# Order of the first loads in a fused attention and gated-unit kernel: tile 1 alone, the value weights in one piece, tiles 2 and 3 together

## The chip, the cores and the metric

The kernel runs on one core of one Trainium2 chip. The metric is the device time of one execution in microseconds (us). A core has TensorE (PE: matmuls; PEld is its weight load), VectorE (DVE), ScalarE (ACT), GpSimd (POOL) and SyncE (SP), which here does nothing but issue transfers (DMA). The engines run their own instruction lists in order and meet at semaphores.

## The reference

One block over 2048 tokens of 512 features, all in bfloat16:

```python
xn = (x - mean(x)) / sqrt(var(x) + 1e-5)                 # per token
q, k, v = split(xn @ wqkv)                               # 32 heads of 16
pq, pk = q @ w_phi, k @ w_phi                            # per head
phi_q = concat(softmax(pq), softmax(-pq))                # phi_k alike from pk
o = (phi_q @ (phi_k.T @ v)) / (phi_q . sum(phi_k) + 1e-6)
out = x + o @ wo + ((xn @ w_gate) * (xn @ w_up)) @ w_down    # 1792 inner features
```

What bears on the change is the beginning: tokens are centred, transposed, and multiplied by the value columns of `wqkv` (columns 1024 to 1535), by `w_gate` and by `w_up`.

## The kernel before, in words

The tokens are 16 tiles of 128 (`NT`), the gated unit works on 4 groups of 4 tiles, with 14 inner tiles each (`units`, line 737). All data lie in one SBUF tensor named `arena`, all matmul results in one PSUM tensor named `ps`, so most rows of the profile have the same names; shapes and times tell them apart.

**The planner.** The program is not written in the order in which it runs. Helpers (`act_op`, `dve`, `pool`, `mms`, `sc.dma`, lines 157 to 307) record steps with an estimated cost, the ranges that they read and write, and a priority. `_order` (line 819) then plays the steps through: on each engine the step that can start first goes first, and steps marked urgent may pass others. The order of each engine's instructions is fixed there, before the kernel runs; semaphore waits are put in by `_emit_all`. For a transfer, the argument `at` (line 157) is the due time in nanoseconds at which the planner takes its data to be there; it is an assumption, and nothing waits for it on the chip. SP issues its transfers in the order that comes out, which for the first loads is the order of the code.

**The first loads** (lines 366 to 380): tile 0 (128 KB), tiles 1 and 2 (256 KB), rows 0 to 255 of the value weights (256 KB), tile 3 (128 KB), rows 256 to 511 of the value weights (256 KB), four of the fourteen columns tiles of gate and up weights (512 KB each), the small head weights, tiles 4 to 7 (512 KB), the key weights by a transposing DMA, five more column tiles of gate and up weights. Ahead of these, ScalarE issues three tiny transfers (`peek`, line 353) that read a few elements of three weight tensors; their data are used nowhere.

**The four start tiles** (`RAW = 4`). The loop at line 757 records for each of tiles 0 to 3:

- `emit_centred` (line 433): the sum of the token's features, and then `512 * x - sum` as centred tokens, without the division by the standard deviation. For tiles 0, 1 and 3 the sum is a VectorE instruction over the two halves of a row (line 443); for the tile in `ACT_MEAN` (tile 2) it is a ScalarE copy with an accumulator (line 437). The subtraction (line 449) is VectorE's: two instructions of 256 columns for tiles 0 and 1, one of 512 for the others.
- `emit_T` (line 494): four TensorE transposes (matmuls against an identity, 128 columns each) in two pairs, each pair copied from PSUM to SBUF by a ScalarE instruction (line 499).
- `emit_moments` and `emit_root` (lines 429 and 455): variance by VectorE (`bn_stats`, `bn_aggr`), and one over the standard deviation by GpSimd. It is applied later, as the scale of ScalarE's copies (`scale_of`).
- `k_pe` (line 574): four value matmuls of 512 columns, one for each quarter of the features. Quarters 0 and 1 read the first half of the value weights, quarters 2 and 3 the second.

While the first tokens are on their way TensorE runs 28 matmuls on constants (line 384), and four more behind tile 0's transposes (line 764).

**Behind the start.** `glu` (line 607) records four gate matmuls and four up matmuls for each of its units; they take tokens of a whole group, so the first of them needs all four start tiles and the gate weights. Then come the key weights' product with the head weights (`wprime(1)`), the key features, the sums over tokens (`emit_kv`), the query side and the output (`final`).

Of the kernel before, what the change touches and what calls it, by code (L numbers as in the profile page):

```python
# [12 lines left out]
PE, ACT, DVE, POOL, SP = "PE", "ACT", "DVE", "POOL", "SP"  # L13
# [168 lines left out]
def bass_parallel_sum__linear_kernel_hedgehog__glu_gated_bilinear__prompt_kernel(  # L182
    nc: bass.Bass,
    A_x: bass.AP,
    A_wqkv: bass.AP,
    A_w_phi: bass.AP,
    A_wo: bass.AP,
    B_x: bass.AP,
    B_w_gate: bass.AP,
    B_w_up: bass.AP,  # L190
    B_w_down: bass.AP,
    out: bass.AP,
):
    with ExitStack() as es:
        _build(nc, es, A_x, A_wqkv, A_w_phi, A_wo, B_w_gate, B_w_up, B_w_down, out)


def _build(nc, es, A_x, A_wqkv, A_w_phi, A_wo, B_w_gate, B_w_up, B_w_down, out):
# [60 lines left out]
    def sbv(name, lo, n):  # L259
        off = layout[name] + lo  # L260
        return arena[:, off:off + n]

    def sbf(name, lo_f32, n_f32):
        off = layout[name]
        return arena[:, off:off + 2 * (lo_f32 + n_f32)].bitcast(F32)[:, lo_f32:lo_f32 + n_f32]
# [21 lines left out]
    def dve(fn, reads, writes, n, rate=1.0, fixed=65.0, prio=None):  # L287
        return sc.step(DVE, fn, reads=reads, writes=writes, cost=fixed + rate * n / 0.96, lat=150.0, prio=prio)
# [31 lines left out]
    def x_tile(t):  # L320
        return sbv("x", t * 512, 512)
# [7 lines left out]
    wv_v = sbv("wv", 0, NQ * 512).rearrange("p (q j) -> p q j", q=NQ)  # L329
# [7 lines left out]
    def load_x(on, t0, n, at):  # L337
        return sc.dma(on, sbv("x", t0 * 512, n * 512).rearrange("p (t d) -> p t d", t=n),
                      x_flat[t0 * 128:(t0 + n) * 128, :].rearrange("(t p) d -> p t d", p=128), at=at)

    def load_w(on, dst, src, at, issue=500.0):
        return sc.dma(on, dst, src, at=at, issue=issue)
# [5 lines left out]
    def load_gu(on, f0, n, at, up=None):  # L348
        return [load_w(on, v[:, :, f0 * 128:(f0 + n) * 128],
                       src[:, f0 * 128:(f0 + n) * 128].rearrange("(q p) f -> p q f", p=128), to)  # L350
                for v, src, to in ((wg_v, B_w_gate, at), (wu_v, B_w_up, up or at))]
# [12 lines left out]
    st = peek(2, every_8th(B_w_up, 0))  # L364

    load_x(SP, 0, 1, 2950.0)
    def load_v(h, at):
        return load_w(SP, wv_v[:, 2 * h:2 * h + 2, :],
                      A_wqkv[h * 256:(h + 1) * 256, 1024:1536].rearrange("(q p) j -> p q j", p=128), at)

    load_x(SP, 1, 2, 3850.0)
    load_v(0, 5050.0)
    load_x(SP, 3, 1, 6100.0)
    load_v(1, 7000.0)
    load_gu(SP, 0, 4, 8300.0, 10600.0)
    sc.dma(SP, wphi_v, bass.AP(tensor=A_w_phi.tensor, offset=A_w_phi.offset, ap=[[16, 128], [2048, NQ], [1, 16]]),
           at=10700.0)
    load_x(SP, 4, 4, 12100.0)
# [45 lines left out]

    RAW = 4

    ACT_MEAN = (2,)

    def emit_moments(t):
        dve(lambda e: e.bn_stats(stats_v[:, t, 0:6], x_tile(t)), [x_tile(t)], [stats_v[:, t, 0:6]], 512)  # L430
# [2 lines left out]
    def emit_centred(t):  # L433

        total = lnt_v[:, 1, 8 + t:9 + t]
        if t in ACT_MEAN:
            sc.step(ACT, lambda e: e.activation(out=xn_tile(t), in_=x_tile(t), func=ACTF.Copy, accum_out=total),
                    reads=[x_tile(t)], writes=[xn_tile(t), total], cost=700.0, lat=180.0)
            again = [xn_tile(t)]
        else:  # L440
            pairs = sbf("tree", (t % 2) * 256, 256)
            lo, hi = x_tile(t)[:, 0:256], x_tile(t)[:, 256:512]
            dve(lambda e: e.scalar_tensor_tensor(out=pairs, in0=lo, scalar=1.0, in1=hi, op0=ALU.mult, op1=ALU.add,  # L443
                                                 accum_out=total), [x_tile(t)], [pairs, total], 256, fixed=150.0)
            again = [pairs]
        n = 256 if t in (0, 1) else 512
        for c in range(0, 512, n):
            o, i = xn_tile(t)[:, c:c + n], x_tile(t)[:, c:c + n]
            dve(lambda e, o=o, i=i: e.tensor_scalar(out=o, in0=i, scalar1=float(D), scalar2=total, op0=ALU.mult,
                                                    op1=ALU.subtract), again + [i, total], [o], n, rate=0.5)  # L450
# [32 lines left out]
    def xn_tile(t):  # L483
        return sbv("xn", (t % 4) * 512, 512)
# [272 lines left out]
    for t in range(RAW):  # L757
        first = len(sc.steps)
        emit_centred(t)
        emit_T(t)  # L760
        for st in sc.steps[first:]:
            st.urgent = True
        if t == 0:
            mms([(bank(3, 0, 128), one, one, True, True)] * 4, cold=True).deps.append(sc.by_eng[PE][-2])
        emit_moments(t)
        emit_root(t)
        k_pe(t)
# [189 lines left out]
```

## Time and profile before

| | |
|---|---|
| runs shown | 219.54, 219.38, 219.1 us; median 219.38 |
| profiled execution | 219.1 us, its span 217.9 us |
| busy share of the span | TensorE 98%, VectorE 86%, ScalarE 59%, GpSimd 5% |
| read from HBM, written | 8.67 MB, 2.10 MB |
| granted TensorE clock | 1.00 |

Times in the profile count from the span's start. A row of the timeline has the start, the duration, the engine, the line, the operation, what it writes and reads, the shapes and how many instructions are merged; in brackets stands how long the engine was idle before it, and what ended the wait. A transfer's time is told from its issue to its landing, the moment at which all its data are there. TensorE's matmuls overlap: one of 512 columns is shown with 0.38 us, and the next one starts 0.216 us after it.

### The profile page before, as it was taken

The page shows a single profiled execution, that of the slowest core. Times are in us where ns is not written, and L with a number is a line of the kernel's source. Part 1 is how long each engine was busy: PE and PEld are TensorE (multiplying, and loading weights), DVE is VectorE, ACT ScalarE, POOL GpSimd, SP SyncE. Part 2 cuts the span into 40 slices and gives each one's busy share as a digit, 9 for nine tenths or more (in the row PEclk, how much of TensorE's full clock was granted, in tenths as well). Part 3 has the DMA queues.
Part 4 walks back from the last instruction along what each step waited for, and adds up shares of the span by engine and source line. Part 5 has one row for each costly group of instructions (what it writes and reads, how often), then busy time and mean ns, then how long its engine had stood idle before and what let it go on. Part 6 is the DMA issues. An engine that isn't in the chain of part 4 may idle for free.

```text
span 217.9 us, 3623 instructions
## 1 busy us (share of the span) xinstructions
PE 213.2 (98%) x1291; PEld 104.4 (48%) x1314; DVE 187.1 (86%) x556; ACT 128.7 (59%) x223; POOL 10.8 (5%) x29
## 2 busy tenths in 40 slices
PE   7999999999999999999999999999999999999996
PEld 6444444444444554444446444444445444454544
DVE  3785999999999549999998799999999999995512
ACT  4668966548553399999884899795254531110000
POOL 2432000110000300000000000000000000000000
PEclk9999999999999999999999999999999999999999
DMA  5994690025900224000000005542681746447321
GB/s 167 321 280 106 164 317 5 0 48 130 350 5 2 47 52 96 0 0 3 0 2 3 2 0 96 76 93 51 122 138 34 167 99 145 97 98 148 90 56 48
DMA packets 47698, 19.92 MB, mean 91 GB/s; under 512 B 37696, under 2 KB 47680, under 8 KB 47680
## 3 DMA queue, kind: packets, MB, share of 16 engines
q1 hardware_dynamic: 47440, 19.69, 37.8%
q8 instruction: 10, 0.16, 0.3%
q14 instruction: 8, 0.07, 0.1%
q10 hardware_dynamic: 240, 0.00, 0.1%
HBM read 8.67 MB, written 2.10 MB: 49 GB/s over the span
## 4 chain that ended last, share of the span: by engine, by line
PE 95%; DMA 2%; SPq 1%; issue 1%; DVE 0%
PE ps L298 95%; DMA arena<-in_A_wqkv_dram 2%; SPq L165 1%; DVE arena L732 0%
## 5 line engine op out<-in xcount | busy, mean ns | idle before, releaser
L298 PE MATMUL ps<-arena 128*128 128x512 bf16 (+5 forms) x1259 | 209.8, 327 | 2.0 <-issue 0.3
L298 PEld LDWEIGHTS ps<-arena 128*128 128x128 bf16 (+1 forms) x1282 | 101.2, 98 | 110.7 <-ACT arena L278 1.6
L278 ACT ACTIVATE arena<-ps 128x512 bf16<-128x512 f32 (+2 forms) x168 | 86.9, 632 | 38.2 <-PE ps L298 26.4
L278 ACT ACTIVATE arena<-arena 128x1024 bf16<-128x1024 bf16 (+1 forms) x40 | 39.6, 1005 | 21.0 <-DVE arena L550 20.8
L564 DVE TENSOR_TENSOR arena<-arena 128x64 f32<-128x64 f32 (+3 forms) x128 | 49.8, 401 | 0.3 <-ACT arena L278 0.2
L544 DVE TENSOR_TENSOR arena<-arena 128x64 bf16<-128x64 bf16 (+3 forms) x128 | 32.0, 276 | 3.8 <-ACT arena L278 3.4
L550 DVE TENSOR_TENSOR arena<-arena 128x1024 bf16<-128x1024 bf16 x32 | 21.7, 680 | 0.1
L625 DVE TENSOR_TENSOR arena<-ps,arena 128x512 bf16<-128x512 f32 x28 | 19.0, 680 | 0.8 <-PE ps L298 0.8
L732 DVE TENSOR_TENSOR arena<-ps,arena 128x512 bf16<-128x512 f32 (+2 forms) x13 | 8.4, 645 | 9.3 <-PE ps L298 9.0
L622 DVE TENSOR_TENSOR arena<-arena 128x512 bf16<-128x512 bf16 x28 | 11.7, 417 | 4.1 <-ACT arena L278 3.9
L596 DVE TENSOR_TENSOR arena<-arena 128x1024 bf16<-128x1024 bf16 x16 | 11.0, 685 | 0.1
L472 DVE BATCH_NORM_STATS2 arena<-arena 128x6 f32<-128x512 bf16 x12 | 8.1, 686 | 1.6 <-DMA arena<-in_A_x_dram 1.6
L278 ACT ACTIVATE arena<-ps,arena 128x512 bf16<-128x512 f32 x12 | 8.0, 682 | 2.1 <-POOL arena L459 1.0
L593 DVE RECIPROCAL arena<-arena 128x64 bf16<-128x64 f32 x16 | 8.8, 549 | 0.0
L694 DVE RECIPROCAL arena<-ps 128x32 f32<-128x32 f32 x16 | 5.6, 348 | 3.3 <-PE ps L298 3.3
L702 DVE TENSOR_TENSOR arena<-ps,arena 128x512 bf16<-128x512 f32 x12 | 8.2, 685 | 0.1
L681 DVE TENSOR_TENSOR arena<-arena 128x512 bf16<-128x512 bf16 x16 | 6.7, 419 | 0.0
L678 DVE RECIPROCAL arena<-arena 128x32 f32<-128x32 f32 x16 | 5.6, 349 | 0.0
L503 DVE TENSOR_SCALAR arena<-arena 128x512 bf16<-128x512 bf16 x12 | 4.2, 408 | 0.9 <-POOL arena L480 0.8
L298 PE MATMUL ps<-const-bfloat16-1.0 128*128 128x128 bf16 x32 | 3.5, 298 | 0.8 <-PEq L942 0.8
L478 POOL TENSOR_SCALAR arena<-arena 128x4 f32<-128x4 f32 x3 | 1.6, 518 | 54.6 <-DVE arena L474 54.6
L443 DVE SCALAR_TENSOR_TENSOR arena<-arena 128x256 f32<-128x256 bf16 x3 | 1.3, 425 | 3.4 <-DMA arena<-in_A_x_dram 3.2
(33 smaller groups left out, 36.0 us busy)
## 6 DMA issues: line engine op xcount, KB each, us to landing
out_dram<-arena SPq DMA_DIRECT2D x15, 128.0 KB, 2.0
arena<-in_B_w_down_dram SPq DMA_DIRECT2D x1, 1792.0 KB, 7.5
arena<-in_B_w_gate_dram SPq DMA_DIRECT2D x2, 640.0 KB, 6.0
arena<-in_B_w_up_dram SPq DMA_DIRECT2D x2, 640.0 KB, 7.9
arena<-in_A_x_dram SPq DMA_DIRECT2D x1, 1024.0 KB, 6.3
arena<-arena SPq DMA_TRANSPOSE x44, 2.6
arena<-in_A_wqkv_dram SPq DMA_DIRECT2D x2, 256.0 KB, 3.8
arena<-in_B_w_gate_dram SPq DMA_DIRECT2D x1, 512.0 KB, 5.3
```

The costliest lines, as they stand in the source:

```text
L278: return e.activation(out=out_ap, in_=in_ap, func=func, scale=scale, **kw)
L298: ins = e.matmul(o, lhsT=l, rhs=r, start=a, stop=z)
L472: dve(lambda e, t=t: e.bn_stats(stats_v[:, t, 0:6], x_tile(t)), [x_tile(t)], [stats_v[:, t, 0:6]], 512)
L544: dve(lambda e, dst=dst, src=src, k=k: e.tensor_tensor(out=dst, in0=src[:, :, 0:k], in1=src[:, :, k:2 * k], op=ALU.max), [src], [dst], 16 ...
L550: dve(lambda e: e.tensor_tensor(out=p4, in0=p4, in1=src[:, :, None, :].to_broadcast([128, 16, 16, 4]), op=ALU.subtract), [pst, src], [pst] ...
L564: dve(lambda e, dst=dst, src=src, k=k: e.tensor_tensor(out=dst, in0=src[:, :, 0:k], in1=src[:, :, k:2 * k], op=ALU.add), [src[:, :, 0:2 * ...
L593: dve(lambda e: e.reciprocal(out=rs, in_=sm), [sm], [rs], 64, rate=6.0)
L596: dve(lambda e: e.tensor_tensor(out=e4, in0=e4, in1=r4[:, :, None, :].to_broadcast([128, 16, 16, 4]), op=ALU.mult), [ek_v[:, t, :], rs], [ ...
L622: dve(lambda e: e.tensor_tensor(out=dst, in0=dst, in1=gr, op=ALU.mult), [dst, gr], [dst], 512, rate=0.5, prio=-1.0)
L625: dve(lambda e: e.tensor_tensor(out=dst, in0=bank(bu), in1=gr, op=ALU.mult), [bank(bu), gr], [dst], 512, prio=-1.0)
L702: dve(lambda e: e.tensor_tensor(out=o4, in0=n4, in1=w4, op=ALU.mult), [nd[:, :, 0:64], w], [o], 512)
L732: dve(lambda e: e.tensor_tensor(out=og, in0=ob, in1=xs, op=ALU.add), [ob, xs], [og], c1 - c0, prio=-2.0)
```

## The change

Three edits, all at the start of the kernel. Tile 1 is loaded by itself behind tile 0; the value weights come behind it in one transfer of 512 KB; tiles 2 and 3 follow in one transfer; the loads behind these keep their order, and their due times are changed. The sum of tile 3 is made by ScalarE and that of tile 2 by VectorE, where it was the other way round. The subtraction of tile 2 is made in two halves.

```diff
     load_x(SP, 0, 1, 2950.0)
-    def load_v(h, at):
-        return load_w(SP, wv_v[:, 2 * h:2 * h + 2, :],
-                      A_wqkv[h * 256:(h + 1) * 256, 1024:1536].rearrange("(q p) j -> p q j", p=128), at)
-
-    load_x(SP, 1, 2, 3850.0)
-    load_v(0, 5050.0)
-    load_x(SP, 3, 1, 6100.0)
-    load_v(1, 7000.0)
-    load_gu(SP, 0, 4, 8300.0, 10600.0)
+    load_x(SP, 1, 1, 3450.0)
+    load_w(SP, wv_v, A_wqkv[:, 1024:1536].rearrange("(q p) j -> p q j", p=128), 5150.0)
+    load_x(SP, 2, 2, 5900.0)
+    load_gu(SP, 0, 4, 8000.0, 9800.0)
...
-    ACT_MEAN = (2,)
+    ACT_MEAN = (3,)
...
-        n = 256 if t in (0, 1) else 512
+        n = 256 if t in (0, 1, 2) else 512
```

TensorE's order changes with it. Before, it was tile 0's transposes, the four matmuls on constants, tile 1's, one value matmul, tile 2's, six value matmuls, tile 3's, and then the remaining nine value matmuls and the first gate and up matmuls. Now it is tile 0's, the four on constants, tile 1's, seven value matmuls, the first two of tile 2's, one value matmul, the other two of tile 2's and tile 3's four, and then the remaining eight value matmuls and the first gate and up matmuls. ScalarE makes its copies of tiles 0 and 1 ahead of the sum of tile 3, where it made the sum of tile 2 ahead of all copies.

## Prediction

> **What bounds the kernel now.** I read the page first: busy shares, the 40 slices, the chain. Fences below copy whole lines.
>
> ```profile
> PE 213.2 (98%) x1291; PEld 104.4 (48%) x1314; DVE 187.1 (86%) x556; ACT 128.7 (59%) x223; POOL 10.8 (5%) x29
> PE   7999999999999999999999999999999999999996
> PE 95%; DMA 2%; SPq 1%; issue 1%; DVE 0%
> ```
>
> TensorE is busy 213.2 of 217.9 us; only the first and last slices are not full. The chain that ended last, in order of time, says where it hands over:
>
> ```profile
> 2.74 4.32 DMA arena<-in_A_wqkv_dram
> 7.07 0.05 issue
> 7.11 8.31 PE ps L298 x70
> 15.42 0.16 issue
> 15.58 10.74 PE ps L298 x49
> ```
>
> Columns are start, duration, what. The second half of the value weights, issued at 2.74, lands at 7.07. From 7.11 TensorE runs in pieces of 49 matmuls in 10.74 us until 216.0, with gaps of 0.05 (two of 0.16). So the kernel is a **start, then a dense block with no slack**: whatever moves the block's first matmuls moves the end by the same amount.
>
> I need the moment at which the four start tiles are done and the first gate matmul begins. Call it G. A 512-column matmul takes (10.74 - 0.38)/48 = 0.216 us, 0.38 being one matmul's own length; a 128-column transpose some 0.056. By TensorE's program order one value matmul stands ahead of tile 2's transposes, six behind them, the sixth of these waiting for the second weight half; then tile 3's four transposes, then the rest. Six of sixteen are issued before 7.11, ten from there: **G before = 7.11 + 10 x 0.216 + 4 x 0.056 = 9.49**. The gate weights landed at 3.22 + 5.3 = 8.5, so they do not set G.
>
> The last views are the timeline of the first 14 us and the transfers:
>
> ```profile
> 3.21 0.43 DVE L443 SCALAR_TENSOR_TENSOR arena<-arena 128x256 f32<-128x256 bf16 x1 [3.21 <-DMA arena<-in_A_x_dram]
> 4.22 0.63 ACT L437 ACTIVATE arena<-arena 128x512 bf16<-128x512 bf16 x1 [0.70 <-DMA arena<-in_A_x_dram]
> 6.34 0.43 DVE L443 SCALAR_TENSOR_TENSOR arena<-arena 128x256 f32<-128x256 bf16 x1
> 6.81 0.35 DVE L449 TENSOR_SCALAR arena<-arena 128x512 bf16<-128x512 bf16 x1
> 7.65 0.66 ACT L278 ACTIVATE arena<-ps 128x256 bf16<-128x256 f32 x2 [1.07 <-PE ps L298]
> ```
> ```profile
> arena<-in_A_wqkv_dram SPq DMA_DIRECT2D x1, 256.0 KB, 4.3
> arena<-in_A_x_dram SPq DMA_DIRECT2D x1, 128.0 KB, 4.1
> ```
>
> The second fence is the transfers in flight of 2.6 to 3.1 us (KB, us to landing): tile 3 and the second weight half. Issue plus landing time gives this list, bytes summed in the queue's order: tile 0 lands at 3.2 (128 KB), tiles 1 and 2 at 4.2 (384), first weight half at 1.72 + 3.2 = 4.9 (640), tile 3 at 2.23 + 4.1 = 6.3 (768), second weight half at 7.07 (1024), gate 8.5 (1536), up 3.73 + 6.5 = 10.2 (2048). The pace is uneven: 256 KB in 0.7 us up to 4.9, then 128 KB in 1.4 us for tile 3, then 512 KB in 1.45 us for the gate weights. The stretches say the same: 320 GB/s in 3 to 4 us, 249 and 239 in 4 to 6, 329 and 347 in 6 to 8.
>
> **The change, part by part.** Let L be the landing of tiles 2 and 3, which now come last of the 1024 KB.
>
> *Tile 1 alone.* Its landing comes from 4.2 to some 3.7 (256 KB lie half-way between 128 at 3.2 and 384 at 4.2). VectorE is at tile 0 until about 4.08 (its halves start 0.20 apart from 3.68), so tile 1's sum starts 0.14 earlier than 4.22. Nothing waits for that; the value weights are later. Worth 0.
>
> *Value weights whole.* 768 KB must land ahead of the first value matmul, where before 640 were enough for six of them. Bounds: 4.9 + 128 KB at the earlier pace of 256 KB in 0.7 = 5.3, and tile 3's 6.3. I take 5.4. Tiles 0 and 1 then run their first seven value matmuls to 5.4 + 7 x 0.216 = 6.9, and TensorE must wait for tile 2: its order has tile 2's first transposes behind the seventh.
>
> *Tiles 2 and 3 last.* This is the new path, step by step from L. Landing to VectorE's sum 0.02 (3.19 to 3.21); sum to first subtraction 0.47 (6.34 to 6.81); half subtraction to transpose 0.35 (tile 1: 4.68 to 5.03); transpose to its copy on ScalarE 0.32 (7.33 to 7.65); copy 0.38; semaphore 0.05 (as the chain's "issue" at 7.07). Sum 1.59: tile 2's first value matmul. Eight of these, 8 x 0.216 = 1.73, lead to G = **L + 3.32**. The rest of tile 2 and tile 3 keeps up: copies follow each other every 0.27, the last ends at L + 2.4, and tile 3's third value matmul stands at L + 2.9.
>
> *Mean of tile 3 on ScalarE, subtraction of tile 2 in halves.* ScalarE's mean takes 0.72 with its read-out (4.22 to 4.94) and is over at L + 0.75; VectorE gets to tile 3's subtraction at L + 0.02 + 0.47 + 2 x 0.20 = L + 0.89. So the mean hides behind tile 2's sum; were that cover gone (mean after the subtraction) it would cost up to 0.72. The halves cost VectorE 0.40 instead of 0.27, +0.13, and give tile 2's first transpose 0.15 earlier; both are in the sum above. ScalarE queues four copies of tiles 2 and 3 behind the mean; the first is needed at L + 1.16, later than its end.
>
> *One DMA issue fewer on SP.* An issue is 0.47 plus 0.04, so everything from the gate weights on is issued 0.5 earlier: gate, up, the head weights, tiles 4 to 7, the transposed key weights. Gate is needed at G, over 0.8 after its 8.5; up is needed at 9.49 + 8 x 0.216 = 11.2, 1.0 after its 10.2; the transposed key weights land at 5.77 + 7.8 = 13.6 for a matmul at 14.8. Covered, so 0 gained, and as the bytes are the same, at most 0.5 lost of that cover.
>
> *Behind G.* Variances start some 0.8 later (VectorE's aggregate of tile 0 goes from 7.15 to L + 1.23), and the scaled value copies with them; their banks are next written by the key-weight product at 14.8 + shift, 2 us after the last copy. 0. The planner also moves four gate/up matmuls ahead of the first batch of 65-column ones, and eight places on ScalarE. TensorE's total work is the same, and the only waits of the dense block are the two of 0.16; I bound this by -0.3 and +0.3 (both of them gone, or two more) and take 0.
>
> **L is the unknown.** Upper bound 7.07: the same 1024 KB as landed then. Lower bound 6.0: 384 KB at 4.2, and the other 640 at the gate weights' 512 KB in 1.45 us, 1.8. Below that stands the planner's own due time for them in the diff, 5.9; its due times before the change are off the landings by -0.34 to +0.36. The slow stretch of 4.9 to 7.07 took 2.15 us for 384 KB against 1.1 at the gate's pace, and it held two new transfers, tile 3's and the half's. After the change it holds one. If each carries part of the loss, L = 6.5 to 7.0; tile 3's share looks the larger, and tile rows are what still comes last. I take **6.7**, a little nearer to 7.07, the row that moved the same bytes. G = 10.02, and 10.02 - 9.49 = **+0.53 us**.
>
> Against the profiled execution, 219.1 us (span 217.9 and 1.2 around it), that is 219.6; the median of the runs shown is 219.38, 0.28 higher, so **219.9**.
>
> The Trainium skill ("DMA: Bandwidth & Descriptors", Rules for kernel authors) advises the reverse of my reading: join many small transfers into large ones, best at 1 MiB and more. By its figure of about 358 GB/s for HBM per core (Specifications) the 640 KB would take an estimated 1.83 us behind 4.2, L = 6.0 and a time 0.2 below before. Here the rows disagree among themselves: the gate weights' 512 KB go at 362 GB/s, tile 3's 128 KB at some 94.
>
> **Rivals.**
> 1. *The joined loads run clean* (not slower). The slow stretch belongs to many short transfers and goes with them: L = 6.0, G = 9.32, -0.17 us: 219.2. For: the gate's pace, and the half before 4.9. Against: tiles 1 and 2 (256 KB in 1.0 us), and that tokens now come where the loss was. It decides from L = 6.62 down: there the time is less than 0.2% (0.44 us, about what a measurement of this kernel tells from no change) above before, and below before from L = 6.17.
> 2. *The slow stretch stays whole*, or the value weights wait in it. L = 7.07 gives G = 10.39, +0.90: 220.3. Weights at 6.3 give 6.35 + 16 x 0.216 + 8 x 0.056 = 10.25 with no wait at all, +0.76. For: the bytes and the time are the same. Against: one transfer start fewer.
> 3. *The gap lets TensorE's pace fall.* Before, its longest wait after 4 us is 0.3; now it may stand idle from 5.3 up to 6.3. The first 28 matmuls start 0.107 apart, later ones 0.056. Were the value matmuls to start at the slow pace, 16 x 0.216 = 3.5 us more: 223. Against: the pace held over the gap ahead of 7.11.
> 4. *A later wait from the new order*, up to 0.3 either way.
>
> **How the numbers follow.** Forecast (L 6.4 to 7.0; 219.6 to 220.2) 0.45; rival 1 with all L below 6.4, 0.25; rival 2, 0.26; rival 3, 0.02; rival 4 deciding, 0.02. Within 0.2%: 0.17 of the forecast (L under 6.62), 0.19 of rival 1, rival 4, together 0.38. Slower: 0.28 + 0.26 + 0.02 = 0.56. Faster needs L under 5.73, or L near 6.0 with a late gain: 0.06 of rival 1. Range: rival 1's 219.2 to 220.4, rival 2 with a little noise; what lies outside has some 0.2.
>
> **What would show it.** In the chain, the hand-over moves from the value weights to tiles 2 and 3: a wait of TensorE for VectorE or ScalarE between 6.5 and 8.5. Tiles 2 and 3 should be seen landing at 6.4 to 7.0 (VectorE's sum behind a DMA), and TensorE's dense block start its gate matmuls 3.3 later. Wrong if that landing is near 6.0 or the gate matmuls start before 9.7; wrong in its mechanism if the hand-over is still the value weights, or if waits show up behind 15 us.

## The result, and the profile after

| | before | after |
|---|---|---|
| median (22 runs each) | 219.16 us | 219.75 us |
| lowest, highest | 218.74, 219.99 | 219.48, 221.85 |
| profiled execution's span | 217.9 us | 218.3 us |
| first gate matmul (G) | 9.50 us | 9.94 us |

The change makes the kernel slower by a little: +0.59 us (0.3%) by the medians; ratio 1.0049, 95% interval 1.0032 to 1.0066, clear of 1. The ratio says 0.5% because it lies near that of the means (220.28 and 219.18): seven of the 22 runs of the changed kernel took 221.3 us or more, none of the 22 before. The other fifteen have a mean of 219.66, +0.48. The prediction said 219.9 us and +0.53. G moved by 0.44 and the span by 0.43, so the whole loss of the profiled execution lies in the first ten microseconds and the dense block hands it on unchanged. Neither G nor the profile tells of the seven late runs; the last section returns to them.

The page of the changed kernel, the lines that answer to the first ones shown of before (busy shares; 40 slices; the chain's shares):

```profile
PE 214.7 (98%) x1314; PEld 104.4 (48%) x1314; DVE 187.0 (86%) x557; ACT 128.9 (59%) x223; POOL 10.0 (5%) x29
PE   7999999999999999999999999999999999999996
PE 97%; DMA 1%; DVE 1%; ACT 0%; issue 0%
```

The picture is the same: a start, then TensorE without slack. The chain of waits (start, duration, what; pieces of 0.02 to 0.07 us between these are left out) shows where the start hands over now:

```profile
4.88 0.30 PE ps L298 x2
5.20 0.67 ACT arena L278 x2
5.94 210.48 PE ps L298 x1274
```

One piece of TensorE from 5.94 to 216.4. This answers the prediction's main question: the hand-over is at the first value matmul, at 5.94, and not at tiles 2 and 3. The chain puts it down to ScalarE's copies, which end at 5.86. But these are tile 1's copies; the first value matmul reads tile 0, whose copies ended at 5.00. It reads the value weights too, and the row of the transfers (KB, us from issue to landing) says when they came:

```profile
arena<-in_A_wqkv_dram SPq DMA_DIRECT2D x1, 512.0 KB, 4.1
arena<-in_A_x_dram SPq DMA_DIRECT2D x1, 256.0 KB, 4.4
```

The weights were issued at 1.71 and landed at 5.81; tiles 2 and 3 were issued at 2.18 and landed at 6.56. Where two releasers end 0.05 apart, the profile names the later one. That it was the weights is settled below, on executions in which the copies had ended 0.3 to 0.4 us earlier. The timeline of the changed kernel has the rest of the start:

```profile
5.94 4.59 PE L298 MATMUL ps<-arena 128*128 128x512 bf16 x26 [0.58 <-ACT arena L278]
6.58 0.63 ACT L432 ACTIVATE arena<-arena 128x512 bf16<-128x512 bf16 x1 [0.72 <-DMA arena<-in_A_x_dram]
6.58 0.43 DVE L438 SCALAR_TENSOR_TENSOR arena<-arena 128x256 f32<-128x256 bf16 x1 [0.77 <-DMA arena<-in_A_x_dram]
7.06 0.74 DVE L444 TENSOR_SCALAR arena<-arena 128x256 bf16<-128x256 bf16 x3
7.76 1.26 ACT L278 ACTIVATE arena<-ps 128x256 bf16<-128x256 f32 x4 [0.46 <-PE ps L298]
```

Both sums start 0.02 behind tiles 2 and 3, ScalarE's for tile 3 beside VectorE's for tile 2, as planned. The seven value matmuls of tiles 0 and 1 end at 7.45; tile 2's first half is ready at 7.40. TensorE does not wait for it.

Why the weights came at 5.81 and not at the 5.4 of the prediction shows in the stretches. First before, then after; the columns are stretch, length, busy time of PE, PEld, DVE, ACT and POOL, granted clock, DMA share, GB/s:

```profile
3.00:4.00 1.00, 0.97 (x10) 0.70 (x7) 0.76 (x4) 0.51 (x1) 0.00 (x0) 1.00 1.00 320
4.00:5.00 1.00, 0.71 (x8) 0.46 (x8) 0.91 (x5) 0.78 (x3) 0.00 (x0) 1.00 0.88 249
5.00:6.00 1.00, 0.97 (x10) 0.70 (x11) 1.00 (x4) 1.00 (x5) 0.00 (x0) 1.00 0.94 239
```
```profile
3.00:4.00 1.00, 0.82 (x10) 0.65 (x7) 0.76 (x4) 0.47 (x1) 0.00 (x0) 1.00 0.78 97
4.00:5.00 1.00, 0.83 (x10) 0.57 (x10) 0.96 (x6) 0.66 (x2) 0.00 (x0) 1.00 1.02 351
5.00:6.00 1.00, 0.42 (x5) 0.20 (x4) 0.82 (x3) 0.66 (x3) 0.00 (x0) 1.00 1.09 382
```

There is a slow stretch as before, but at another place, and shorter and deeper. Before, 4 to 6 us were slow, at tile 3 and the second weight half. After, it is one stretch of 97 GB/s at 3 to 4 us, just where the queue's turn comes to the value weights (tile 1, ahead of them, landed at 3.53). At that stretch's pace before (320) its bytes would have come some 0.6 us earlier (an estimate: 223 KB at 370 GB/s), and the weights at 5.2.

### The profile page after: what moved, and what is told of

It is laid out like the page before. It is cut to its first block, busy times and chain, and to the rows that moved or that the text cites. A ratio compares the mean times of both kernels' runs of the same rounds, so it can differ in the third digit from the quotient of the medians.

```text
span 218.3 us, 3645 instructions
## 1 busy us (share of the span) xinstructions
PE 214.7 (98%) x1314; PEld 104.4 (48%) x1314; DVE 187.0 (86%) x557; ACT 128.9 (59%) x223; POOL 10.0 (5%) x29
## 4 chain that ended last, share of the span: by engine, by line
PE 97%; DMA 1%; DVE 1%; ACT 0%; issue 0%
PE ps L298 97%; DMA arena<-in_A_x_dram 1%; DVE arena L438 0%; DVE arena L444 0%; ACT arena L278 0%; DVE arena L727 0%
## 5 line engine op out<-in xcount | busy, mean ns | idle before, releaser
L298 PEld LDWEIGHTS ps<-const-bfloat16-1.0 128*128 128x128 bf16 x32 | 3.1, 140 | 0.8 <-issue 0.8
```

What stands on the lines that cost most here:

```text
L298: ins = e.matmul(o, lhsT=l, rhs=r, start=a, stop=z)
```

## Experiments

Two readings stood against each other after the result. **Weights' theory**: G = W + 4.13, W being the landing of the weights (0.13 to the first value matmul, 16 x 0.216, 8 x 0.056, and 0.09 of waiting for ScalarE's copy). **Tiles' theory**, the prediction's: G = L + 3.32, L being the landing of tiles 2 and 3. In the profile above the first gives 5.81 + 4.13 = 9.94 and the second 6.56 + 3.32 = 9.88, 0.06 from what was measured; one profile can't tell them apart. This table has what the profiled executions showed (us; n in brackets):

| kernel | W | L | G | G - W | median | ratio, 95% interval |
|---|---|---|---|---|---|---|
| changed | 5.81 | 6.56 | 9.94 | 4.13 | 219.75 (22) | 1.0049, 1.0032 to 1.0066 |
| e1 changed, again | 6.07 | 6.82 | 10.20 | 4.13 | 220.04 (9) | 1.0055, 1.0033 to 1.0077 |
| e12 changed, third time | 6.15 | 6.91 | 10.28 | 4.13 | 219.88 (12) | 1.0040, 1.0016 to 1.0064 |
| e2 loads only | 6.05 | 6.81 | 10.62 | 4.57 | 220.47 (6) | 1.0070, 1.0045 to 1.0094 |
| e3 sums and halves only | 7.11 | | 9.92 | | 219.62 (12) | 1.0030, 1.0012 to 1.0048 |
| e4 gap filled | 6.22 | 6.90 | 10.35 | 4.13 | 219.97 (5) | 1.0034, 1.0022 to 1.0046 |
| e5 changed, no peeks | 6.12 | 6.87 | 10.25 | 4.13 | 219.87 (11) | 1.0048, 1.0026 to 1.0069 |
| e6 weights in halves | 6.02 | 8.62 | 11.96 | | 219.80 (11) | 1.0038, 1.0021 to 1.0055 |
| e11 the same again | 6.11 | 6.80 | 10.14 | 4.03 | 219.76 (12) | 1.0020, 1.0004 to 1.0037 |
| e7 short warm-up | 6.09 | 6.83 | 11.79 | | 221.36 (6) | 1.0109, 1.0089 to 1.0128 |
| e8 interleaved | 6.99 | 7.34 | 10.19 | | 220.23 (5) | 1.0055, 1.0042 to 1.0068 |
| e9 tiles 2, 3 apart | 6.20 | 6.89 | 10.33 | 4.13 | 220.22 (12) | 1.0056, 1.0029 to 1.0084 |
| e10 before, no peeks | 7.05 | | 10.00 | | 219.37 (12) | 1.0005, 0.9985 to 1.0024 |

W is the last landing of the value weights where they come in two transfers, and L that of tile 3 where tiles 2 and 3 come apart. The kernel before, run beside them, had medians of 219.18 (e1 to e4), 219.22 (e5 to e8) and 219.20 (e9 to e12). A ratio is made from runs of one chip; a profile's G is one execution, and W varies by 0.34 between executions of the same kernel (5.81, 6.07, 6.15). G of e6, e7 and e10 holds things that are told at each: a straggling part, the slow pace, late gate weights.

### e1: the changed kernel again

No edit.

> The changed kernel once more, for a second profile and more times. Path theory: tiles 2 and 3 land at L near 6.5 and the gate matmuls start at L + 3.4, near 9.9, 0.4 later than before; ratio 1.002 to 1.005. Some executions of the changed kernel were near 221.5 while most were near 219.6; before had none. Clock theory: in those TensorE had an idle gap of 0.6 us ahead of the first value matmul and ran the value matmuls at the slow pace (0.43 us from start to start); about a third of the executions lie near 221.5 again, and if the profiled one is among them the slow pace shows behind the gap. Transfer theory: in those the value weights land about 2 us later and the pace is 0.216 as ever.

The second execution separates the two releasers. Its chain, and its waits (total, times, longest):

```profile
1.70 4.37 DMA arena<-in_A_wqkv_dram
...
6.21 1.78 PE ps L298 x9
```
```profile
PE ps L298 <- DMA arena<-in_A_wqkv_dram: 0.7, 1, 0.7
```

Now the weights land at 6.07, 0.08 later than the end of ScalarE's copies (5.99), and the first value matmul follows 0.14 behind them, where it was 0.13 behind 5.81. In e5, e9 and e12 the copies end at 5.75 to 5.81, the weights land at 6.12 to 6.20, and the first value matmul again follows them by 0.14. The hand-over is the value weights. G is 4.13 behind them again.

### e2 and e3: one part alone

e2 takes the changed kernel's loads and keeps the old sums and halves; e3 the reverse.

```diff
 # e2, against the changed kernel
-    ACT_MEAN = (3,)
+    ACT_MEAN = (2,)
...
-        n = 256 if t in (0, 1, 2) else 512
+        n = 256 if t in (0, 1) else 512
 # e3, against the kernel before
-    ACT_MEAN = (2,)
+    ACT_MEAN = (3,)
...
-        n = 256 if t in (0, 1) else 512
+        n = 256 if t in (0, 1, 2) else 512
```

> Only the loads are changed; tile 2's sum stays on ScalarE and tile 3's on VectorE, subtractions of tiles 2 and 3 whole. Path theory: tile 2's first transpose now waits for ScalarE's sum (0.74 against VectorE's 0.47) and for a whole subtraction (0.35 against 0.20), so gate matmuls start at L + 3.7 to 3.8 instead of L + 3.4: 0.3 to 0.4 slower than the full change. Rival, that TensorE's own work sets it behind the late value weights: as the full change within 0.1.

> Only the sums and the halves are changed, the loads are as before. Path theory: tile 3 lands at 6.3, its ScalarE sum ends near 7.1, its transposes come near 7.5, while TensorE has eight value matmuls from 7.07 to 8.8 to do: hidden, the same as before within 0.15 us. Rival, that moving a sum to ScalarE costs by itself: 0.3 us or more slower.

With the new loads the old sums are worse: G = 10.62 at the weights' landing of e1, where e1 has 10.20, so the swap of sums and the halves gain 0.42 here. The timeline of e2 shows TensorE without its next tile:

```profile
9.11 2.10 PE L298 MATMUL ps<-arena 128*128 128x512 bf16 x9 [0.59 <-ACT arena L278]
```

With the old loads the same two edits cost as much: G 9.92 against 9.50. That was not expected ("the same as before within 0.15"); the rival set beside it, 0.3 us or more, came true. In e3 tile 2's sum waits on VectorE for tile 1's subtraction (it starts at 5.21; before, ScalarE had it at 4.22), so tile 2's transposes start at 6.01 where they started at 5.56, and only five value matmuls, not six, are done before the second weight half. And tile 3's sum sits on ScalarE behind tile 2's copies, though its data were there at 6.34:

```profile
5.58 1.46 ACT L278 ACTIVATE arena<-ps 128x256 bf16<-128x256 f32 x4 [0.57 <-PE ps L298]
6.94 0.62 ACT L437 ACTIVATE arena<-arena 128x512 bf16<-128x512 bf16 x1
7.69 0.35 DVE L449 TENSOR_SCALAR arena<-arena 128x512 bf16<-128x512 bf16 x1
```

So the parts don't add: by G the loads alone cost 1.1 (e2), the sums and halves alone 0.4 (e3), both together 0.7 (e1, on the same chip). The swap repairs what the loads break.

### e4 and e7: does the gap cost TensorE's pace?

e4 puts twelve more constant matmuls into the gap before the first value matmul, all other orders alike; e7 halves the 28 constant matmuls at the kernel's beginning.

```diff
 # e4, against the changed kernel, in the start loop
+        n_pe = len(sc.by_eng[PE])
         k_pe(t)
+        if t == 0:
+            first_v = sc.by_eng[PE][n_pe]
+        if t == 1:
+            fill = mms([(bank(3, 0, 128), one, one, True, True)] * 12)
+            fill.deps.append(sc.by_eng[PE][n_pe - 1])
+            fill.cost = 1.0
+            first_v.deps.append(fill)
 # e7, against the changed kernel
-    mms([(bank(3, 0, 128), one, one, True, True)] * 28, cold=True)
+    mms([(bank(3, 0, 128), one, one, True, True)] * 14, cold=True)
```

> The changed kernel with twelve matmuls on constants (128 columns, 0.056 each, 0.67 us) between tile 1's transposes and the first value matmul; all engines' orders are otherwise those of the changed kernel. Clock theory: no execution near 221.5 any more, the others unchanged within 0.1 (the fill ends near 5.9, when the value weights land). Transfer theory: as many near 221.5 as without the fill. Path theory says nothing of the group near 221.5 and expects the rest at 219.6.

> The changed kernel with 14 matmuls on constants at the start in place of 28; orders are otherwise the same. TensorE is idle from 2.3 to 4.0. Clock theory: the transposes and the value matmuls run at the slow pace (0.107 and 0.43 from start to start) in most executions, until some 3.4 us of full work have passed; the gate matmuls start 1.5 to 2.5 later, so most executions lie at 221.3 to 222.2, where some of the changed kernel's lie. Transfer theory: no change of pace, the same mixture of 219.7 and 221.5 as with 28.

e4 gains nothing in the median: 219.97 against 220.04 for e1 on the same chip, G = W + 4.13 again. Twelve matmuls over 5.19 to 6.05 changed no later pace: in e1, too, the value matmuls behind the gap start 0.216 apart. In e7 they do not. Its timeline of TensorE:

```profile
3.93 0.61 PE L298 MATMUL ps<-arena 128*128 128x128 bf16 x4 [1.45 <-DVE arena L444]
...
6.22 5.94 PE L298 MATMUL ps<-arena 128*128 128x512 bf16 x24 [0.83 <-DMA arena<-in_A_wqkv_dram]
```

Here the value matmuls start 0.427 us apart from 6.22 to about 9.4 and 0.216 apart from there, and the median is 1.5 above e5's and 1.6 above e6's, both on the same chip. The transposes ahead of the gap (3.93 to 5.08) are at the slow pace too, 0.107 apart: the pace did not fall in the gap, it had not yet risen. So the price that the prediction's third rival feared exists; in the profiles it comes with a shorter warm-up, not with this gap. The Trainium skill ("TensorE: Matmul & The Clock Gate", Part 1) puts the half pace down to a clock gate that opens after some 3.4 us of sustained activity. The trace of e7 agrees: the pace changes some 3.2 us behind the point where TensorE's work becomes dense. The traces with 28 constant matmuls, the first of them at 0.83, spread wider: in the changed kernel the pace rises at 3.54, 2.7 us behind it; in e1 the transposes up to 5.2 are still 0.107 apart, and in e8 value matmuls still start 0.43 apart at 5.65 and 6.08, 5.2 us behind the first, with no pause above 0.2 us between. When the pace rises is thus not settled by the number of constant matmuls alone. In these profiles a late rise cost nothing, since the value weights were what TensorE waited for.

### e5 and e10: the tiny transfers at the beginning

The three peeks are removed, in the changed kernel (e5) and in the kernel before (e10).

```diff
-    st = peek(0, every_8th(A_wqkv, 1024))
-    st = peek(1, every_8th(B_w_gate, 0))
-    st = peek(2, every_8th(B_w_up, 0))
```

> The changed kernel without ScalarE's three tiny transfers, whose data nothing uses. In every profile of the changed loads the transfers move only 60 to 120 GB/s from 3.0 to 4.0 us, as the value weights begin, and 370 GB/s afterwards. Disturbance theory, that the tiny transfers (in flight until 4.9) cause it: the slow stretch goes, value weights land near 5.0, L near 5.8, gate matmuls near 9.2: 0.7 faster than the changed kernel and 0.3 faster than before. First-touch theory, that a weight tensor's first reads are slow whoever makes them: the slow stretch stays or grows, and new ones show where the gate and up weights begin; L at 6.6 or later, no gain.

> The kernel before without the three tiny transfers. If they are of no use, as with the changed loads, landings stay within 0.2 and so does the time, or it is up to 0.2 faster, tiles 0 and 1 landing 0.2 earlier. If early reads do make a weight tensor's later reads faster: the first half of the value weights (no slow stretch at 3.5 before) shows one, some 0.5 later, and the time is 0.3 or more slower.

If the peeks disturbed the first reads, the slow stretch should go; if they had made later reads of the same tensors quicker, new slow stretches should come at the gate and up weights. In e5 neither came. Its stretch:

```profile
3.00:4.00 1.00, 1.00 (x13) 0.85 (x10) 0.96 (x5) 0.00 (x0) 0.00 (x0) 1.00 0.50 59
```

59 GB/s without any peek, the weights at 6.12, and the times those of the changed kernel. In e10 the first weight half landed at 4.69 (before: 4.92), and the ratio is 1.0005 with an interval on both sides of 1. Its gate weights came late, at 9.95, but so did e11's (9.84), which has the peeks. Both theories of the peeks fall; what slows this stretch stays open.

### e6 and e11: the value weights in two halves again, at their new place

```diff
-    load_w(SP, wv_v, A_wqkv[:, 1024:1536].rearrange("(q p) j -> p q j", p=128), 5150.0)
+    for h, at in ((0, 5149.0), (1, 5150.0)):
+        load_w(SP, wv_v[:, 2 * h:2 * h + 2, :],
+               A_wqkv[h * 256:(h + 1) * 256, 1024:1536].rearrange("(q p) j -> p q j", p=128), at)
```

> The changed kernel with the value weights in two transfers of 256 KB, one right behind the other, in the place of the one; all engines' orders but SP's are the same. Path theory: the first half lands 0.4 to 0.7 earlier and some value matmuls with it, but L stays within 0.2 and the gate matmuls start at L + 3.4: the same as the changed kernel within 0.2 us. Joining theory, that the single transfer itself costs (its slow beginning): L earlier by 0.3 or more and the time with it. Clock theory: a shorter gap ahead of the first value matmul, fewer executions near 221.5.

> The kernel with the value weights in two transfers once more, beside the changed kernel of the same call, for a profile and the share of late executions. Straggler theory for the executions near 221.5: in the one profiled so far one part of tiles 2 and 3's transfer came 1.9 us after the other fifteen, and TensorE waited 2.1 us for tile 2 at the full pace; so if this profile is of a time under 220.3, tiles 2 and 3 land at 6.5 to 6.9 and the gate matmuls start at L + 3.3 to 3.4 although the first half of the weights landed near 5.1. Time under 220.3: as the changed kernel within 0.2.

This is the test of the tiles' theory: take the weights' wait away, and tiles 2 and 3 must bind. In e11 the halves land at 4.80 and 6.11, L is 6.80, and its timeline has the wait that the prediction had looked for in the changed kernel:

```profile
6.83 0.42 DVE L440 SCALAR_TENSOR_TENSOR arena<-arena 128x256 f32<-128x256 bf16 x1 [1.08 <-DMA arena<-in_A_x_dram]
7.64 1.15 PE L298 MATMUL ps<-arena 128*128 128x128 bf16 x9 [0.15 <-DVE arena L446]
```

G is 10.14, that is L + 3.34, against the 3.32 of the prediction. So the tiles' path was priced rightly and ends just ahead of the weights': at equal landings it is worth some 0.1 only, and the halves gain next to nothing in the median (219.76 against 219.88 for e12 on the same chip, 0.12; the intervals overlap).

The slow stretch does change with the halves: 3 to 4 us move 219 GB/s in e11 and 194 in e6, where the eight profiles with the weights in one transfer have 59 to 105. But 4 to 5 us are then at 228 and 215 instead of 299 to 362, and by 6 us the bytes are much the same (775 KB from 3 us on in e11, 751 in e12). So the deep beginning belongs to the one large transfer, as the joining theory had it, and dividing it only spreads the loss: W (6.02 and 6.11) and L (6.80 in e11) stay within the changed kernel's own spread.

e6, the same program, was profiled in an execution of 221.6 us, the slowest of its eleven. The chain shows one thing out of place:

```profile
2.69 5.93 DMA arena<-in_A_x_dram
8.64 0.45 DVE arena L440 x2
9.11 0.30 DVE arena L446
9.46 0.28 PE ps L298 x2
```

Tiles 2 and 3 land at 8.62. The transfer's end is marked in sixteen parts; fifteen were there by 6.70 and the last at 8.62. TensorE waits 2.1 us, and its matmuls keep 0.216 apart. A straggling part, not the pace, makes this execution late. In the gate and up weights behind it one part again comes 1.9 and 1.7 us after the other fifteen (10.10 and 11.57).

### e8: tokens and weights interleaved

Tile 0, tile 1, first weight half, tile 2, second half, tile 3; all sums on VectorE, all subtractions in halves.

```diff
 # against the kernel before
-    load_x(SP, 1, 2, 3850.0)
+    load_x(SP, 1, 1, 3450.0)
     load_v(0, 5050.0)
-    load_x(SP, 3, 1, 6100.0)
-    load_v(1, 7000.0)
-    load_gu(SP, 0, 4, 8300.0, 10600.0)
+    load_x(SP, 2, 1, 5500.0)
+    load_v(1, 6200.0)
+    load_x(SP, 3, 1, 6600.0)
+    load_gu(SP, 0, 4, 8300.0, 10200.0)
...
-    ACT_MEAN = (2,)
+    ACT_MEAN = ()
...
-        n = 256 if t in (0, 1) else 512
+        n = 256 if t in (0, 1, 2, 3) else 512
```

> An order meant to be faster: tile 0, tile 1, first half of the value weights, tile 2, second half, tile 3; all sums on VectorE and all subtractions in halves. Path theory: first half lands near 5.2, the second near 6.2, tile 3 last at L near 6.6 to 6.9; but now only one tile hangs on the last landing: L + 1.6 for its first value matmul and 4 x 0.216 behind, L + 2.5; and TensorE's own work from 5.2 on is 16 x 0.216 + 8 x 0.056 = 3.9. Gate matmuls at 9.2 to 9.5, before at 9.5: 0 to 0.3 faster than before. Rival, one more transfer start makes the slow stretch longer: tile 3 after 7.2, slower than before.

It is no better: 220.23, ratio 1.0055, and G = 10.19 where 9.2 to 9.5 were expected. The stretches tell why:

```profile
4.00:5.00 1.00, 1.00 (x10) 0.80 (x10) 0.96 (x6) 0.60 (x2) 0.00 (x0) 1.00 0.80 241
5.00:6.00 1.00, 1.00 (x7) 0.48 (x5) 1.00 (x3) 0.71 (x3) 0.00 (x0) 1.00 0.89 235
6.00:7.00 1.00, 0.73 (x3) 0.15 (x1) 0.57 (x4) 0.00 (x0) 0.00 (x0) 1.00 0.84 240
```

Some 240 GB/s for three microseconds on end, where the changed kernel has 351, 382 and 364. The second half lands at 6.99 and tile 3 at 7.34 (the rival of the expectation: "after 7.2"), and the up weights at 11.46, for which TensorE waits another 0.3.

### e9: tiles 2 and 3 in two transfers

```diff
-    load_x(SP, 2, 2, 5900.0)
+    load_x(SP, 2, 1, 5899.0)
+    load_x(SP, 3, 1, 5900.0)
```

> The changed kernel with tiles 2 and 3 in two transfers of 128 KB; all orders but SP's are the same. In the changed kernel two paths end nearly together: the weights' (they land at W; first value matmul W + 0.14, sixteen of them and eight transposes 3.9, gate matmuls at W + 4.04) and the tiles' (L + 3.32), with L = W + 0.75. Tie theory: tile 2 lands 0.3 to 0.4 earlier, the tiles' path drops out, and the gate matmuls start at W + 4.04 to 4.08 instead of W + 4.13: 0.05 to 0.1 us faster, too little to be told. Tiles-alone theory, by which tile 2's landing sets the end: 0.3 faster. Against both: one transfer more may bring W or L later.

Tile 2 lands at 6.56, 0.33 ahead of tile 3. By the tiles' theory alone G would be 6.56 + 3.32 = 9.88. It is 10.33, W + 4.13: nothing gained, the weights bind. The 0.05 to 0.1 that the tie theory expected did not come either, so the 0.09 of waiting for ScalarE's copy belongs to the weights' path (TensorE's order has tile 2's transposes behind the seventh value matmul) and not to the landing of the tiles. (Its median of 220.22 holds four of the late executions of the last section; the other eight lie between 219.51 and 220.42.) The timeline says so at the first value matmul:

```profile
6.34 2.65 PE L298 MATMUL ps<-arena 128*128 128x512 bf16 x16 [1.04 <-DMA arena<-in_A_wqkv_dram]
```

### e12: the changed kernel a third time

No edit; beside e9, e10 and e11 on the same chip.

> The changed kernel a third time, beside the others of this call. A quarter of its executions near 221.5 and the rest near 219.8. Straggler theory: if the profiled one is near 221.5, one of the first transfers lands 1.5 to 2.1 later than in the profiles at 219.6 to 219.8 (5.8 and 6.6 there for weights and tiles), with matmuls 0.216 apart. Clock theory: landings as ever, matmuls 0.43 apart.

G is again 4.13 behind the weights (6.15, 10.28). No kernel of this study beat the one before.

## Why the prediction was right in size and wrong in its path

**The frame held.** A start, a dense block without slack, so that G's shift is the span's shift: +0.44 and +0.43.

**The failing step is "Value weights whole ... I take 5.4".** They landed at 5.81, and at 6.05 to 6.22 in the later profiles. The value taken lay 0.1 above its lower bound (5.3: 128 KB at the pace ahead of 4.9), which assumes that the slow stretch stays where it was, with tile 3. The runs showed it at the beginning of the weights. The prediction had the right shape as the second half of rival 2, weights that wait in the slow stretch. It priced their path at W + 3.95; the runs show W + 4.13 (0.13 from landing to first matmul instead of 0.05, and 0.09 of waiting for ScalarE's copy at tile 2's first value matmul).

**Beside it stands a misread pace.** The list of landings gave tile 3 "128 KB in 1.4 us", some 94 GB/s, and 384 KB in 2.15 us. That was not what the queue moved: the stretches before have 249, 239 and 329 GB/s there. A landing is the last of sixteen parts. Of tile 3 fourteen were there by 5.45 and the last two at 6.18 and 6.32, while the second weight half's first part came at 5.75. Two late parts set tile 3's landing; after the change all sixteen of tiles 2 and 3 come between 5.98 and 6.56.

**So the forecast's mechanism was wrong by its own test**: the hand-over is still the value weights, and TensorE's wait between 6.5 and 8.5 never came. What saved the size is luck: the two paths nearly tie, and L came 0.14 earlier than taken. With W = 5.4 the weights' path would have ended at 9.53; with L at 6.56 the tiles' path ends at 9.88; the first profile has 9.94. The time of 219.9 rests besides on a before of 219.38, the median of three runs; that of 22 is 219.16.

**Tiles 2 and 3 last: right.** L was 6.56 (6.7 taken), and the sum of 3.32 was confirmed by e11 within 0.02. It is second by 0.05 to 0.13 in the changed kernel's profiles and e4's and e5's.

**Mean of tile 3 on ScalarE, halves of tile 2: right here.** The mean hides beside tile 2's sum (both start at 6.58). e2 measures what the two edits are worth with these loads, 0.42; e3 that they cost 0.42 with the old ones. The prediction had not asked that second question; it took their merit as theirs and not as the loads'.

**Tile 1 alone, one DMA issue fewer, everything behind G: 0, right.** Tile 1 landed at 3.53 and TensorE waited for the weights behind it all the same. The gate weights landed at 8.05, the up weights at 9.77, each before its use, and no new wait shows behind 15 us. One reading was off without harm: in the changed kernel's order the up weights are needed four matmuls behind G and not eight (in e11, with G = 10.14 and the up weights landing at 11.32, the fifth starts at 11.36 instead of 11.00).

**Rival 1**, clean loads, failed: the joined loads are quick once under way (382 GB/s), but their beginning is not. The rule of the Trainium skill weighed there ("DMA: Bandwidth & Descriptors", Rules for kernel authors: join transfers) finds half a case here: e8, with more transfer starts, ran at 240 GB/s; but e11, which splits the 512 KB in two, was not slower than e12. **Rival 3** failed in the profiles: behind gaps of 0.58 to 1.04 us the pace is 0.216 in every one with 28 constant matmuls. Whether it holds in the late executions, none of which was profiled with such a gap, is open (last section).

**Not settled**: what slows 3 to 4 us. It is not the peeks, and in two transfers the loss spreads (e11). Bytes may be the better account: from 3 to 6 us before moved 320 + 249 + 239 = 808 KB and after 97 + 351 + 382 = 830, so the new order changed who pays for a loss of much the same size. That is an observation and no cause.

## What to carry to other kernels

When a slow stretch is seen among the first loads, ask for whom it will be slow after the reorder, and price every order with the loss put on the load that the bottleneck waits for. When two paths tie within 0.1 us, fixing one shows only the other: name both landings and both sums, and test each by taking its rival's wait away (e9 and e11). Where an edit repairs what another breaks, its worth is a property of the pair, and only the two half-changes on the chip tell it (e2 and e3).

## What the runs showed of the hardware that was not expected

- Some executions come some 2 us late, above 220.8 and up to 222.2. Of the kernels that load the value weights as 512 KB (changed, e1, e12, e2, e4, e5, e9) 20 of 77 runs did; of those with two transfers of 256 KB (e3, e6, e8, e10, e11) 2 of 52, and of the kernel before 1 of 97. e7, late throughout, is left out of this count. It is no small matter: the changed kernel's mean over its 22 runs is 0.5 above its median.
- Why they are late is open, and two readings stand. *A straggler*: e6's late execution, the only one profiled, had one, and the pace was 0.216. *The pace*, which is rival 3: two of the changed kernel's seven late runs (221.85 both, span 220.6) list a granted clock of 0.992, and no other run with a listed clock is below 1.00. That is 0.8% of the span, 1.8 us (an estimate), against a span 2.3 longer than the profiled one. The other late runs list 1.00, but so do all six of e7, which ran at the slow pace and whose median, 221.36, lies among the late times. What the clock theory expected of e4 (none late with the gap filled: 0 of 5), of e6 (fewer with a shorter gap: 1 of 11, and 0 of 12 in e11) and of e7 came out, though e4's five runs prove little. A late execution of the changed kernel, profiled, would tell.
- What a straggler costs depends on who is waiting. In e10 thirteen parts of the gate weights are there by 8.49 and the last at 9.95, 0.5 behind the moment at which TensorE is ready for them. Its waits:

```profile
PE ps L298 <- DMA arena<-in_B_w_gate_dram: 0.4, 1, 0.4
```

  In e11 they landed at 9.84 against 8.05 in the changed kernel, and as G was 10.14 nobody waited for them; the up weights behind them came late as well (11.32), and for these TensorE waited 0.2.
- Leaving out 14 of the 28 constant matmuls cost about 1.5 us (e7): the largest effect of the study, from work whose result is used nowhere. The profile's granted clock reads 1.00 throughout, but the trace's first entry for it stands at 9.43, where the pace rises; ahead of that, only the distance from one matmul to the next tells it.
